# Recurrent attention and expert layer on one core: where the first group's small steps run, and when the second group's x is made

## The chip, the cores and the metric

The kernel runs on one core of a Trainium2 chip. Its time is the device time of one execution in microseconds, the median of several runs. The engines are TensorE (PE in the profile, with its weight loads as PEld), VectorE (DVE), ScalarE (ACT), GpSimd (POOL) and SyncE (SP, which here only issues DMAs). Each takes its instructions in order.

## The reference

```python
def _attn_ref(q, k, v, alpha):               # (4, 8, 768, 48) each
    ...
    for t in range(S):
        state = alpha[:, :, t, :, None] * state + np.einsum('bhd,bhe->bhde', k[:, :, t], v[:, :, t])
        y[:, :, t] = np.einsum('bhd,bhde->bhe', q[:, :, t], state)

def _moe_ref(x, domain_probs, w1, w2):       # x (3072, 384), 4 experts, F = 1024
    p = domain_probs / (domain_probs.sum(-1, keepdims=True) + 1e-09)
    for e in range(E):
        h = np.maximum(x @ w1[e], 0.0)
        out += p[:, e:e + 1] * (h @ w2[e])
```

x is the attention's y with heads side by side, (batch, position) as rows. Everything is float32.

## The kernel before

The 768 positions of each of the 4 batches are cut into 6 blocks of 128, which gives 24 units, taken block by block: unit u is block u // 4 of batch u % 4. Units are put together into groups whose x feeds the expert layer at once: the first group holds units 0 and 1, the second units 2 to 5, and so on in fours, with two left for the last. For each group, four experts are run; each has an `up` stage (x times w1, in eight chunks of 128 hidden columns) and a `down` stage (hidden times w2). The attention of the next group's units is dealt out between these matmuls: `deal` gives each of a unit's steps (the stretches between `yield`s) a due time by a table of costs, and `advance` emits the steps that are due. The emission order is the order on each engine.

A unit (`attention`) first transposes alpha, k and q on TensorE (`turned`, L270). ScalarE copies the first two out of PSUM as AT (L281) and KT (L286); VectorE multiplies the third by AT into QT (L293). `own` and `dot` (L289, L290) are the terms of each position with itself. Then come seven levels, m = 1, 2, 4 ... 64. At each, ScalarE copies one half of QT into a block of its own, qb (`copy_q`, L312, two instructions); VectorE multiplies that half by the decay of its neighbour (`next_q`, L319) and makes the next level's decay (L321); and `next_k` makes the next level's K: the right halves are copied unchanged (L330, ScalarE), the left halves are multiplied by the decay (L331, VectorE). There are six such copies a unit. The K tiles rotate over five buffers. TensorE's `products` (L338) give the scores of a level, which VectorE puts into `near` under a mask (L348); `far` (L393) is the last level. ScalarE copies both into `lat` (L406 for far, L410 for near, two instructions each, one for each half of the partitions). `result` (L432) multiplies lat by v, adds the state's part where there is an earlier block, and leaves x; `turn_keys` (L456) and the state's update (L467 to L476) follow.

From the second group on, x is taken in three parts, top, low and dif, so that matmuls of a faster type can be used. `split_x` makes them, at four points of the last `down` before the group's first `up`: step 0 makes all the top parts on ScalarE (L502), and steps 1 to 3 make low and dif of one third each on VectorE (`split_rest`, L252 and L253). The points are shares of that `down`: 0.0, 0.6, 0.7 and 0.78. Beside the first group the weights are split likewise (`split_piece`, L226 to L232) and the parts stored to DRAM by DMAs from GpSimd's queue (L233); `load_piece` reads them back for later groups (L196) and reads the raw weights (L214, L215 for w1, L217 for w2), all on SP's queue. GpSimd has no other work behind the memsets of the start but the stores of finished rows (L675).

At the start, SP's queue issues unit 0's loads (alpha, k, q and three for v), unit 1's, and the first four pieces of w1. ScalarE's queue issues the identity, the masks and the probabilities `p_all`. TensorE runs fillers, matmuls of zeros that nobody reads (L749): eight before the first step, and then so many behind each step of units 0 and 1 as the list in the code says. `norm_probs` follows at the end of that list.

Of the kernel before, what the change touches and what calls it, by code (L numbers as in the profile page):

```python
# [10 lines left out]
F32 = mybir.dt.float32  # L11
# [5 lines left out]
AX = mybir.AxisListType  # L17
# [3 lines left out]
def kernel(  # L21
# [37 lines left out]
    nc = tc.nc  # L59

    B, H, S, D = q.shape
    E, DM, F = moe_w1.shape
    P = 128
# [7 lines left out]
    NT = B * P  # L71
# [11 lines left out]
    n = np.arange(QUAD)[None, :]  # L83
# [7 lines left out]
    work = ctx.enter_context(tc.tile_pool(name="work", bufs=2))  # L91
# [7 lines left out]
    p_all = const.tile([P, NBLK, E], F32, name="p_all")  # L99
# [3 lines left out]
    near = const.tile([P, H, HALF], F32, name="near")  # L103
    lat = const.tile([P, H, P], F32, name="lat")
# [7 lines left out]
    half = B // 2  # L112
# [18 lines left out]
    def raw(u, nm):  # L131
        return values[u % 2] if nm == "v" else apart[nm] if u == 1 else early[nm]
# [27 lines left out]
    def load(u, names):  # L160
        if u >= len(units):
            return
        cb, b = units[u]
        for nm in names:
            src = srcs[nm][b, :, cb * P:(cb + 1) * P, :].rearrange("h s d -> s h d")
            if nm != "v":
                nc.sync.dma_start(out=raw(u, nm)[:, :, :D], in_=src)
                continue

            pairs = raw(u, nm).rearrange("p (a i) d -> p a i d", i=2)  # L170
            src = src.rearrange("p (a i) d -> p a i d", i=2)
            nc.sync.dma_start(out=pairs[:, :, 0, :D], in_=src[:, :, 0])
            nc.sync.dma_start(out=pairs[:, :, 1, :TAIL], in_=src[:, :, 1, QUAD:])
            nc.sync.dma_start(out=pairs[:, :, 1, TAIL:D], in_=src[:, :, 1, :QUAD])
# [81 lines left out]
    def norm_probs():  # L256
        nc.vector.reduce_sum(out=tot, in_=p_all, axis=AX.X)
        nc.vector.tensor_scalar_add(out=tot, in0=tot, scalar1=1e-9)
        nc.vector.reciprocal(out=tot, in_=tot)
        nc.vector.tensor_mul(p_all, p_all, tot.unsqueeze(2).broadcast_to([P, NBLK, E]))  # L260
        nc.vector.tensor_scalar_mul(out=p_fine, in0=p_all, scalar1=FINE)


    def halves(t, m):
        return t.rearrange("p a (b two r) -> p a b two r", two=2, r=m)

    def turned(src):
        tp = ps.tile([P, NP, P], F32, name="tp", tag="w")
        for p in range(NP):
            nc.tensor.transpose(tp[:, p, :], src(p), ident)  # L270
        return tp

    def attention(u):
        cb, b = units[u]
        ra, rk, rq, rv = (raw(u, nm) for nm in ("a", "k", "q", "v"))
# [6 lines left out]
        after = u + 2 if u == 0 else u + 1 if u > 1 else len(units)  # L282
# [1 line left out]
        yield  # L284
        KT = keys()
        nc.scalar.copy(out=KT, in_=turned(pair(rk)))  # L286
        own = work.tile([P, NT], F32, name="t")[:, :H * D].rearrange("p (h d) -> p h d", d=D)
        dot = work.tile([P, H], F32, name="dot")
        nc.vector.tensor_mul(own, rq[:, :, :D], rk[:, :, :D])  # L289
        nc.vector.reduce_sum(out=dot, in_=own, axis=AX.X)  # L290
        load(after, "k")
        yield
        nc.vector.tensor_mul(QT, turned(pair(rq)), AT)  # L293
        load(after, "q")
        yield

# [27 lines left out]
        def next_k(li):  # L324
            m = LEVELS[li]
            old = new = halves(KTs[li], m)
            if li + 1 < len(LEVELS):
                KTs.append(keys())
                new = halves(KTs[-1], m)
                nc.scalar.copy(out=new[:, :, :, 1, :], in_=old[:, :, :, 1, :])  # L330
            nc.vector.tensor_mul(new[:, :, :, 0, :], old[:, :, :, 0, :],  # L331
                                 spread(halved(decs[li])[:, :, :, 1], m))

# [23 lines left out]
        for li in range(3):  # L357
            copy_q(li)
            next_q(li)
            next_k(li)  # L360
            yield
# [6 lines left out]
        for li in range(4):  # L368
            products(li, banks[li // 2][:, li % 2])
        next_q(3)  # L370
        next_k(3)
        take(0, banks[0][:, 0])
        take(1, banks[0][:, 1])
        yield
        copy_q(4)
        next_q(4)
        next_k(4)
        take(2, banks[1][:, 0])
        take(3, banks[1][:, 1])
# [24 lines left out]
        for s in range(2):  # L404
            rows = slice(HALF * s, HALF * (s + 1))
            nc.scalar.copy(out=parts[:HALF, :, s, :, HALF:], in_=far[rows])  # L406
        yield
        for s in range(2):
            rows = slice(HALF * s, HALF * (s + 1))
            nc.scalar.copy(out=lat[rows, :, rows], in_=near[rows])  # L410
        KT = KTs[-1]
        yield

# [49 lines left out]
        if cb < NCB - 1:  # L463
# [5 lines left out]
            for i in range(2):  # L469
                rows = slice(HD * i, HD * (i + 1))  # L470
                old, add = st[rows, :, i, :], sps[rows, :, i, :]
# [208 lines left out]
    def cost(layer, gi, e):  # L680
        n = len(groups[gi]) / 4
        if layer == 0:
            return 2.1 * n if split1(gi, e) else 2.6 * n
        return 4.1 if gi > 1 else 4.7 if split2(gi, e) else 5.4
# [32 lines left out]
    def advance(spent):  # L717
        nonlocal clock
        clock += spent
        while waiting and clock >= waiting[0][0]:  # L720
            next(waiting.popleft()[2], None)

    with tc.manual_schedule():
        nc.scalar.dma_start(out=ident_all, in_=nc.inline_tensor(ident_np, name="ident_c").ap())
        nc.scalar.dma_start(out=masks, in_=nc.inline_tensor(mask_np, name="masks_c").ap())
        nc.scalar.dma_start(out=p_all, in_=moe_domain_probs.rearrange("(n p) e -> p n e", p=P))
        nc.gpsimd.memset(sts[B - 1], 0.0)
        for nm in "akq":
            for r in (early[nm], apart[nm]):
                nc.gpsimd.memset(r[:, :, D:], 0.0)  # L730
        nc.gpsimd.memset(lat[HALF:, :, :HALF], 0.0)
        for t in values + blocks:
            nc.gpsimd.memset(t, 0.0)
        for t in sts[:-1]:
            nc.gpsimd.memset(t, 0.0)

        load(0, "akqv")
        load(1, "akqv")
        for i in range(NQ):
            load_piece(0, i)  # L740

        idle = ps.tile([P, P], F32, name="idle", tag="g", bufs=4)
        zeros = sts[B - 1].rearrange("p a i d -> p (a i d)")[:, :P]

        def fill(n):
            for _ in range(n):
                nc.tensor.matmul(idle, lhsT=zeros, rhs=zeros, start=True, stop=True)  # L749

        runs = [attention(u) for u in range(len(groups[0]))]
        fill(8)
        for u, n in ((0, 3), (0, 6), (0, 4), (0, 5), (0, 5), (0, 4), (0, 3), (1, 0), (0, 0), (0, 2),
                     (0, 2), (1, 2), (0, 2), (1, 0), (0, 0), (0, 4), (0, 4), (0, 0)):
            next(runs[u])
            fill(n)
        norm_probs()

        span = cost(0, 0, 0) * FCH / 2 + cost(1, 0, 0)
        waiting.extend((span * (k + 1) / 15, u, runs[u])  # L760
                       for k, u in enumerate([1, 1, 1, 0, 1, 0, *[1] * 8]))
        for fc in range(FCH):
            up(0, 0, fc, slice(0, 1))
            advance(cost(0, 0, 0) / 2)
        down(0, 0, [0], deque())
        while waiting:
            next(waiting.popleft()[2], None)
        clock = 0.0
        waiting.extend((1.0 + k, 1, runs[1]) for k in range(2))
        waiting.extend(deal())  # L770

        for (gi, e), after in zip(tasks, [*tasks[1:], (None, None)]):
            rest = gi == e == 0
            for fc in range(FCH):
                up(gi, e, fc, slice(1, len(groups[0])) if rest else None)
                advance(cost(0, gi, e) / (2 if rest else 1))
            each = len(groups[gi]) if split2(gi, e) else 1
            turns = [range(k, k + each) for k in range(rest, len(groups[gi]), each)]
            for k, slots in enumerate(turns):

                between = deque()
                if after[1] == 0:
                    for step, at in enumerate((0.0, 0.6, 0.7, 0.78)):
                        at = at * len(turns) - k
                        if 0 <= at < 1:
                            between.append((at, lambda step=step: split_x(after[0], step)))
                down(gi, e, slots, between)
        while stores:
            stores.popleft()()
# [28 lines left out]
```

## Time and profile before

| | us |
|---|---|
| median of 8 runs | 1063.61 |
| lowest, highest | 1060.66, 1064.84 |
| the profiled execution | 1063.43 |
| its span, first to last instruction | 1061.7 |
| mean granted TensorE clock | 0.998 |

The span is what the profile's tables are made of; the profiled execution's own time is 1.73 us longer. A line of the profile that begins with an engine (or with the time) names the source line, the operation, what is written and what is read, and how often; in square brackets is the idle time of the engine just before it, with what ended it. Matmuls of float32 show up as two instructions each.

| of the span | busy us | share |
|---|---|---|
| PE | 1041.1 | 98% |
| PE's weight loads | 905.7 | 85% |
| DVE | 781.1 | 74% |
| ACT | 568.6 | 54% |
| POOL | 32.7 | 3% |

### The profile page before, as it was taken

The page shows a single profiled execution, that of the slowest core. Times are in us where ns is not written, and L with a number is a line of the kernel's source. Part 1 is how long each engine was busy: PE and PEld are TensorE (multiplying, and loading weights), DVE is VectorE, ACT ScalarE, POOL GpSimd, SP SyncE. Part 2 cuts the span into 40 slices and gives each one's busy share as a digit, 9 for nine tenths or more (in the row PEclk, how much of TensorE's full clock was granted, in tenths as well). Part 3 has the DMA queues.
Part 4 walks back from the last instruction along what each step waited for, and adds up shares of the span by engine and source line. Part 5 has one row for each costly group of instructions (what it writes and reads, how often), then busy time and mean ns, then how long its engine had stood idle before and what let it go on. Part 6 is the DMA issues. An engine that isn't in the chain of part 4 may idle for free.

```text
span 1061.7 us, 21599 instructions
## 1 busy us (share of the span) xinstructions
PE 1041.1 (98%) x8508; PEld 905.7 (85%) x8508; DVE 781.1 (74%) x1619; ACT 568.6 (54%) x1202; POOL 32.7 (3%) x71
## 2 busy tenths in 40 slices
PE   8899999999999999999999999999999999999998
PEld 8777776687878798898898998988989889898988
DVE  5488777677779877778877877986878776666565
ACT  5687875675756555536446535555564543423232
POOL 2010010000001000000000000000000000000000
PEclk9999999999999999999999999999999999999999
DMA  8596699797877958658669558585694554544531
GB/s 124 158 326 208 237 314 350 275 347 240 303 253 274 379 174 285 274 158 328 235 197 362 194 205 333 165 320 222 173 363 173 209 209 152 205 179 179 192 166 45
DMA packets 158837, 251.66 MB, mean 237 GB/s; under 512 B 120112, under 2 KB 135344, under 8 KB 136208
## 3 DMA queue, kind: packets, MB, share of 16 engines
q1 hardware_dynamic: 149600, 208.82, 57.4%
q0 software_dynamic: 5760, 41.29, 9.7%
q8 instruction: 67, 1.10, 0.4%
q10 hardware_dynamic: 3376, 0.17, 0.3%
q14 instruction: 34, 0.28, 0.1%
HBM read 207.79 MB, written 42.47 MB: 236 GB/s over the span
## 4 chain that ended last, share of the span: by engine, by line
PE 85%; DVE 5%; ACT 5%; DMA 2%; issue 2%; SPq 0%; ACTq 0%; DVEq 0%
PE ops L639 36%; PE one L546 23%; PE two L546 11%; PE sc L338 6%; PE yps L432 3%; PE tp L270 3%; ACT qb L312 2%; PE one L538 2%; PE sps L467 1%; PE far L393 1%; DMA hT<-in_moe_w_dram 1%; DVE near L348 1%; DVE w L230 1%; ACT KT L330 1%; DMA rq<-in_q_dram 1%
## 5 line engine op out<-in xcount | busy, mean ns | idle before, releaser
L639 PE MATMUL ops<-w,hT 128*128 128x384 f32 x1872 | 346.4, 340 | 0.2 <-DVE hT L592 0.2
L639 PEld LDWEIGHTS ops<-w,hT 128*128 128x128 f32 x1872 | 324.3, 188 | 4.7 <-ACT t L557 0.6
L546 PE MATMUL one<-xT,w 128*128 128x512 f32 x960 | 253.9, 399 | 2.7 <-DVE xT L252 2.3
L546 PEld LDWEIGHTS one<-xT,w 128*128 128x128 f32 x960 | 176.2, 189 | 41.9 <-DVE xT L252 4.0
L557 ACT ACTIVATE t<-one 128x512 f32<-128x512 f32 (+1 forms) x192 | 107.0, 557 | 179.9 <-PE one L546 174.9
L312 ACT COPY qb<-QT 64x256 f32<-64x256 f32 x336 | 136.6, 406 | 71.1 <-DVE QT L293 42.5
L586 DVE SCALAR_TENSOR_TENSOR hT<-t,hT 128x512 fp32r<-128x512 f32 (+1 forms) x172 | 110.4, 642 | 68.3 <-ACT hT L584 66.1
L559 DVE TENSOR_TENSOR t<-t,two 128x512 f32<-128x512 f32 (+1 forms) x172 | 109.3, 636 | 57.8 <-ACT t L557 29.3
L584 ACT ACTIVATE hT<-t 128x512 fp32r<-128x512 f32 (+1 forms) x172 | 101.8, 592 | 86.3 <-DVE t L559 85.3
L546 PE MATMUL two<-xT,w 128*128 128x512 f32 x480 | 136.8, 393 | 0.0
L546 PEld LDWEIGHTS two<-xT,w 128*128 128x128 f32 x480 | 90.4, 189 | 20.1 <-DVE acc L668 0.2
L639 PE MATMUL ops<-hT 128*128 128x384 f32 x288 | 100.9, 491 | 0.4 <-DMA hT<-in_moe_w_dram 0.4
L592 DVE SCALAR_TENSOR_TENSOR hT<-hT 128x512 fp32r<-128x512 f32 (+1 forms) x172 | 100.9, 633 | 0.0
L348 DVE COPY_PREDICATED near<-masks,sc 128x256 f32<-128x256 uint8 x144 | 76.8, 533 | 19.4 <-PE sc L338 16.7
L319 DVE TENSOR_TENSOR QT<-QT,dec 128x256 f32<-128x256 f32 x144 | 60.8, 422 | 36.0 <-ACT qb L312 35.3
L338 PEld LDWEIGHTS sc<-qb,KT 128*64 128x64 f32 x2304 | 72.7, 138 | 9.3 <-issue 4.7
L338 PE MATMUL sc<-qb,KT 128*64 128x64 f32 x2304 | 77.2, 223 | 2.6 <-ACT qb L312 2.6
L639 PEld LDWEIGHTS ops<-hT 128*128 128x128 f32 x288 | 52.1, 190 | 29.8 <-DMA hT<-in_moe_w_dram 1.1
L668 DVE SCALAR_TENSOR_TENSOR acc<-ops,p_all,acc 128x384 f32<-128x384 f32 x82 | 49.9, 614 | 30.2 <-PE ops L639 29.1
L330 ACT COPY KT<-KT 128x256 f32<-128x256 f32 x144 | 60.0, 416 | 3.2
L331 DVE TENSOR_TENSOR KT<-KT,dec 128x256 f32<-128x256 f32 x144 | 60.1, 418 | 0.0
L538 PE MATMUL one<-xT,w 128*128 128x256 f32 (+1 forms) x240 | 46.2, 340 | 0.6 <-ACT xT L448 0.6
(88 smaller groups left out, 935.4 us busy)
## 6 DMA issues: line engine op xcount, KB each, us to landing
w<-kept SPq DMA_DIRECT2D x144, 1152.0 KB
kept<-w POOLq DMA_DIRECT2D x32, 1152.0 KB, 7.3
hT<-in_moe_w_dram SPq DMA_DIRECT2D x32, 384.0 KB
w<-in_moe_w_dram SPq DMA_DIRECT2D x48, 128.0 KB
ra<-in_alpha_dram SPq DMA_DIRECT2D x23, 192.0 KB
rk<-in_k_dram SPq DMA_DIRECT2D x23, 192.0 KB
rq<-in_q_dram SPq DMA_DIRECT2D x23, 192.0 KB
out_dram<-acc POOLq DMA_DIRECT2D x18, 192.0 KB, 7.6
```

Of the source, the lines that this page charges most:

```text
L312: nc.scalar.copy(out=qb[rows, :, i, :].rearrange("p a (b r) -> p a b r", r=m), in_=qv[rows])
L330: nc.scalar.copy(out=new[:, :, :, 1, :], in_=old[:, :, :, 1, :])
L338: nc.tensor.matmul(out[HALF * s:HALF * (s + 1), 2 * p:2 * p + 2, :], lhsT=KTs[li][:, p, HALF * s:HALF * (s + 1)], rhs=qbs[li][:, p, :, QUA ...
L348: nc.vector.copy_predicated(near.rearrange("p a (b two r) -> p a b two r", two=2, r=m)[:, :, :, 1, :], mk.unsqueeze(1).broadcast_to([P, H, ...
L538: nc.tensor.matmul(one, lhsT=w[:, kc], rhs=xraws[gi][:, kc, lo:hi], start=(kc == 0), stop=(kc == KC - 1))
L546: nc.tensor.matmul(out, lhsT=w[:, part, kc], rhs=x_part(gi, part, kc), start=(part == terms[0] and kc == 0), stop=(part == terms[-1] and k ...
L557: nc.scalar.activation(out=t, in_=one, func=ACT.Copy, scale=FINE)
L559: nc.vector.tensor_add(t, t, two)
L584: nc.scalar.activation(out=top, in_=x, func=ACT.Relu, scale=TRIM)
L586: nc.vector.scalar_tensor_tensor(out=low, in0=x, scalar=0.0, in1=top.bitcast(F32), op0=ALU.max, op1=ALU.subtract)
L592: nc.vector.scalar_tensor_tensor(out=dif, in0=top.bitcast(F32), scalar=1 / 4096.0, in1=low.bitcast(F32), op0=ALU.mult, op1=ALU.subtract)
L639: nc.tensor.matmul(sums[at], lhsT=h, rhs=w, start=(n == begins[at]), stop=(n == ends[at]))
```

## The change

Six edits. In the first unit (`alone`), own and dot are emitted behind QT and not ahead of it, with the load of k for a later unit that follows them, and the second of lat's two copies of near goes to VectorE. For units 0 to 5 (`dense`: those that run ahead of or beside the first group), the copy of K's right halves goes from ScalarE to GpSimd. The load of p_all goes from ScalarE's queue to SP's, behind the loads of units 0 and 1 and ahead of the first pieces of w1. The fillers are 7, 2 and 3 instead of 8, 3 and 6 at the first three places. And steps 1 to 3 of `split_x` come at 0.3, 0.42 and 0.54 of the first group's last `down`; for later groups they stay where they were.

```diff
         dot = work.tile([P, H], F32, name="dot")
-        nc.vector.tensor_mul(own, rq[:, :, :D], rk[:, :, :D])
-        nc.vector.reduce_sum(out=dot, in_=own, axis=AX.X)
-        load(after, "k")
+        def own_terms():
+            own = work.tile([P, NT], F32, name="t")[:, :H * D].rearrange("p (h d) -> p h d", d=D)
+            nc.vector.tensor_mul(own, rq[:, :, :D], rk[:, :, :D])
+            nc.vector.reduce_sum(out=dot, in_=own, axis=AX.X)
+            load(after, "k")
+        alone = u == 0
+        dense = u < half + B
+        if not alone:
+            own_terms()
         yield
         nc.vector.tensor_mul(QT, turned(pair(rq)), AT)
+        if alone:
+            own_terms()
         load(after, "q")
...
-                nc.scalar.copy(out=new[:, :, :, 1, :], in_=old[:, :, :, 1, :])
+                copy = nc.gpsimd.tensor_copy if dense else nc.scalar.copy
+                copy(out=new[:, :, :, 1, :], in_=old[:, :, :, 1, :])
...
-            nc.scalar.copy(out=lat[rows, :, rows], in_=near[rows])
+            copy = nc.vector.tensor_copy if alone and s else nc.scalar.copy
+            copy(out=lat[rows, :, rows], in_=near[rows])
...
-        nc.scalar.dma_start(out=p_all, in_=moe_domain_probs.rearrange("(n p) e -> p n e", p=P))
...
         load(0, "akqv")
         load(1, "akqv")
+        nc.sync.dma_start(out=p_all, in_=moe_domain_probs.rearrange("(n p) e -> p n e", p=P))
         for i in range(NQ):
             load_piece(0, i)
...
-        fill(8)
-        for u, n in ((0, 3), (0, 6), (0, 4), (0, 5), (0, 5), (0, 4), (0, 3), (1, 0), (0, 0), (0, 2),
+        fill(7)
+        for u, n in ((0, 2), (0, 3), (0, 4), (0, 5), (0, 5), (0, 4), (0, 3), (1, 0), (0, 0), (0, 2),
                      (0, 2), (1, 2), (0, 2), (1, 0), (0, 0), (0, 4), (0, 4), (0, 0)):
...
-                    for step, at in enumerate((0.0, 0.6, 0.7, 0.78)):
+                    for step, at in enumerate((0.0, 0.3, 0.42, 0.54) if gi == 0 else
+                                              (0.0, 0.6, 0.7, 0.78)):
```

More of the change, by code (lines that the diff above doesn't have):

```diff
@@ L286, in attention @@
         nc.scalar.copy(out=KT, in_=turned(pair(rk)))
-        own = work.tile([P, NT], F32, name="t")[:, :H * D].rearrange("p (h d) -> p h d", d=D)
         dot = work.tile([P, H], F32, name="dot")
-        nc.vector.tensor_mul(own, rq[:, :, :D], rk[:, :, :D])
-        nc.vector.reduce_sum(out=dot, in_=own, axis=AX.X)
-        load(after, "k")
+        def own_terms():
[7 more added lines that the diff above has]
+            own_terms()
         yield
         nc.vector.tensor_mul(QT, turned(pair(rq)), AT)
+        if alone:
+            own_terms()
         load(after, "q")
```

## The prediction

> **What bounds the kernel now.** The page's first part comes first: TensorE is busy for 98% of the span, so the question is where the missing 20 us lie. The table by stage (columns: window and length, PE, PEld, DVE, ACT, POOL busy with instruction counts, granted clock, DMA share, GB/s), with its limits at the first matmul of the expert layer, at the end of the first group and after the second group's start, answers it.
>
> ```profile
> PE 1041.1 (98%) x8508; PEld 905.7 (85%) x8508; DVE 781.1 (74%) x1619; ACT 568.6 (54%) x1202; POOL 32.7 (3%) x71
> ```
> ```profile
> 0.00:26.36 26.36, 22.36 (x269) 21.20 (x269) 13.93 (x39) 14.02 (x30) 5.92 (x21) 1.00 0.84 124
> 26.36:60.00 33.64, 29.94 (x297) 24.52 (x298) 19.40 (x44) 23.29 (x58) 1.53 (x3) 1.00 0.66 181
> 60.00:163.80 103.80, 97.60 (x999) 75.22 (x998) 81.72 (x183) 80.67 (x178) 7.13 (x15) 1.00 0.83 277
> 163.80:176.00 12.20, 10.37 (x36) 7.21 (x35) 9.13 (x20) 4.40 (x10) 1.06 (x2) 0.86 0.97 374
> 176.00:1061.70 885.70, 880.79 (x6913) 777.56 (x6911) 656.92 (x1335) 446.18 (x928) 17.10 (x32) 1.00 0.65 236
> ```
>
> After 176 us TensorE idles 4.9 of 886 us, and the change touches nothing there: whatever is won before 176 us should arrive whole at the end. Before it, 4.0 us are idle in the first 26.36 us (where part of the busy time is the filler of L749, too), 3.7 + 6.2 us in the rest of the first group, and 1.8 us at the second group's start, at a mean granted clock of only 0.86.
>
> Next, the timeline of the start, on TensorE and VectorE. It shows what the first unit waits for.
>
> ```profile
> 1.21 3.78 PE L749 MATMUL idle<-st 128*128 128x128 f32 x16 [1.21 <-POOL st L727]
> 4.78 1.06 PE L270 MATMUL tp<-ident,ra 128*128 128x128 f32 x4
> 6.35 0.60 PE L270 MATMUL tp<-ident,rk 128*128 128x128 f32 x4
> 6.79 1.50 PE L749 MATMUL idle<-st 128*128 128x128 f32 x12
> 8.80 0.63 PE L270 MATMUL tp<-ident,rq 128*128 128x128 f32 x4 [0.51 <-DMA rq<-in_q_dram]
> ...
> 8.77 0.56 DVE L289 TENSOR_TENSOR t<-rq,rk 128x384 f32<-128x384 f32 x1 [8.77 <-DMA rq<-in_q_dram]
> 9.83 0.68 DVE L293 TENSOR_TENSOR QT<-tp,AT 128x512 f32<-128x512 f32 x1
> ```
>
> The transposes of ra and rk follow the filler without a gap; that of rq waits for its load. The product QT at L293 then waits a little more, for own and dot (L289, L290) ahead of it on VectorE.
>
> Last, TensorE's timeline at the second group's start, and the clock there.
>
> ```profile
> 165.99 0.49 PE L546 MATMUL one<-xT,w 128*128 128x512 f32 x1 [0.18 <-DVE xT L252]
> 167.31 0.51 PE L546 MATMUL one<-xT,w 128*128 128x512 f32 x1 [0.83 <-DVE xT L252]
> 168.64 1.34 PE L546 MATMUL one<-xT,w 128*128 128x512 f32 x4 [0.82 <-DVE xT L252]
> ```
> ```profile
> 168.00:170.00 2.00, 1.36 (x5) 0.89 1.01 424
> 170.00:172.00 2.00, 2.00 (x8) 0.50 1.02 431
> 172.00:174.00 2.00, 2.00 (x8) 0.76 0.99 279
> ```
>
> Three stalls on the pieces of x add to 1.83 us, and right after them the granted clock is at half.
>
> **The change, part by part.** The sum is made against the profiled execution's own 1063.43 us (span 1061.7); the median of the runs is 1063.61, 0.18 above it.
>
> 1. *p_all leaves ACT's queue; fewer fillers; own and dot behind QT.* p_all is 128 x 24 = 3,072 rows of 16 bytes, most of the 3,376 packets of q10. The DMA view of 0 to 10 us counts 9,123 packets, with the engines saturated from 1.75 us: 0.90 us a thousand. p_all therefore takes 2.8 us of the engines while rq is on its way; without it rq could land at 8.77 - 2.8 = 6.0. If the queues did not share the engines, it would gain nothing. TensorE's fillers then gate: one fewer of the first eight saves 0.25 to 0.47 (3.78 / 8; I take 0.4), one of three 0.25, three of six 0.75 (1.50 / 2). The rq transposes start at 8.80 - 0.51 - 1.40 = 6.9 at the earliest, 1.9 us sooner. QT could have begun at 9.5, when its transposes were done, but began at 9.83: another 0.33. Sum -2.23, and between -0.33 and -2.5. What it moves: own and dot (0.56 + 0.55) run while ACT copies qb for 0.86 us and VectorE sat idle for 0.98, so they cost nothing; uncovered they'd cost 1.1. On SP's queue the issue of k's load for the third unit stays between those of a and q. p_all's issue now stands ahead of twelve issues of w1; by DMA time these move back 2.8 us at the end of the same saturated stretch that p_all leaves shorter, so they land as before. The last was issued at 23.15 and its piece is read by the seventh of eight chunks, near 31 us: covered by some 4 us even with a start 2.5 us sooner.
>
> 2. *lat's second half on VectorE (first unit).* ACT's two copies of L410 take 1.25 us together from 23.38. VectorE does its half behind the KT product that ends at 23.66, so near 24.2 both are done. But the eight fillers ahead of yps end at 24.37, where yps began at 24.68: -0.3.
>
> 3. *GpSimd's 36 KT copies.* Each took ACT 0.41 us (0.33 from start to start) and lies in ACT's queue in front of what TensorE waits for. The PE waits between 20 and 180 us name ACT:
>
> ```profile
> PE yps L432 <- ACT lat L410: 3.1, 4, 1.4
> PE far L393 <- ACT qb L312: 2.9, 2, 1.6
> PE sc L338 <- ACT qb L312: 2.6, 3, 1.2
> ```
>
> In ACT's timeline a KT copy stands in the unbroken row just ahead of the awaited copy in five of the long ones (those that end at 33.0, 63.6, 80.2, 84.0 and 121.3 us): 5 x 0.33 = -1.65. The far waits are set by VectorE (qb 6 waits for QT), and gain nothing. If the row ahead merely re-forms it is half, -0.8; if each earlier copy helps too, up to -3.
>
> Against it stands GpSimd's own price p. No row shows a GpSimd copy. Its memsets give 204 ns for 128x128 and 540 ns for 128x512, so some 0.32 for 256 columns that are only written; twice that, 0.64, if reading is added in full. ACT needs 0.41. I take p = 0.5. Nor does a row show VectorE beside a reading GpSimd: memsets end before VectorE's first instruction. So the blocking is between zero and all of p that no idle time covers. Copy 0 needs only the transposed K. Copies 4 and 5 lie beside the near updates (1.49 and 0.89 us). Copies 1 and 2 end in the 0.3 us that VectorE waits for qb, and cost up to p - 0.3 each; copy 3 has no such gap, up to p: 0.9 us a unit. On the path that counts whole for the first two units and, by my estimate, a quarter for each of the four others, which have matmuls to cover them: up to 3 x 0.9 = 2.7. I take half: +0.45 at the start and +0.9 beyond it.
>
> The rule that speaks against this part is in the Trainium skill, SBUF — State Buffer, section "Who interferes with whom": a VectorE instruction with two SBUF inputs and a GpSimd instruction that reads SBUF exclude each other. The QT, dec and KT products are of that kind; by the rule the blocking is the whole 2.7 and the result 1.35 us later than my sum, by the rows alone anything from zero. No run so far shows it.
>
> On POOL's queue the copies share with the weight stores of L233, which wait there for VectorE's L232 (76.3 us of waits in five of them). A KT copy behind such a store waits for it plus its 0.53 us issue. VectorE's next KT product comes 1.2 us after L232 (QT, dec and KT go first), so the cover holds for p up to 0.7.
>
> 4. *x from 0.30.* The pieces come one turn earlier. VectorE's 3 x (0.68 + 0.69) us are the same work, moved from 165.25 to some 156 to 163 us. ACT's top part is ready at 156.2. VectorE idles 0.53 and 0.91 us there. The unit's own work slides behind, into the time the pieces leave free. TensorE arrives at 165.8 and finds all three: -1.83 of stalls. What is slow behind them is counted by rows: four transposes take 1.06 us (0.60 elsewhere, from start to start 0.42 more), six matmuls of one 2.19 (1.56), three of two 1.49 (0.86): -1.68. Together -3.5; if only the stalls go, -1.8.
>
> Sum: -2.23 - 0.3 + 0.45 - 1.65 + 0.9 - 3.5 = -6.3. 1063.43 - 6.3 + 0.18 = **1057.3**.
>
> **Rivals.** *Slower: GpSimd's copy is long, and VectorE waits for each.* The gains without blocking are 2.53 + 1.65 + 3.5 = 7.7 us. Blocking costs 3 x (2(p - 0.3) + p) = 9p - 1.8, so it decides from p = 1.06 us on. At p = 1.5 it is 11.7, and the kernel 4 us slower: 1067.6. For it: strided elements in runs as short as one. Against it: p would be three times the interpolated memset. 9%.
>
> *The transfers hold the time.* SP's queue issues without a break from 139.4 to 189 us at a DMA share near 1:
>
> ```profile
> 155.61 17.53 SPq L196 DMA_DIRECT2D w<-kept  x4
> 174.55 5.32 SPq L217 DMA_DIRECT2D hT<-in_moe_w_dram  x2
> ```
>
> The fourth w piece, issued by 173.1, is read at 184.5; w2's last, issued by 182.5, after 195. With some 3 us from issue to landing (my estimate; POOL's stores of the same size took 7.3 in all) 5 us or more are left, hardly 2 after moving the readers up by 3.5. Were there none, part 4 is lost: 1060.8; if the earlier gain is absorbed too, 1063.6. 16%.
>
> *rq does not land sooner*, because another transfer in the same queue held it. Part 1 shrinks to 0.33, the sum to -4.4: 1059.2. 12%.
>
> **How the numbers follow.** The forecast has 63%. A difference of 0.2%, 2.1 us, is about what this kernel's runs can tell from no change. Its own bounds reach from -9.3 (1054.3) to about -0.5 (part 1 alone failing with full blocking and only the stalls won). 1053.8 to 1061.8 takes in the third rival, most of the forecast and half of the second. Faster: 0.61 + 0.12 + 0.08 = 0.81; within 0.2%: 0.02 + 0.08 = 0.10; slower 0.09.
>
> **What would show it.** Right: rq's transposes near 6.9, QT near 7.6, the first matmul of L538 near 24.3 us; no xT wait, and clock 1.00, at the second group's start, which lies near 163.0 instead of 165.99. GpSimd rows of about 0.5 us, VectorE's L319 starting 0.1 to 0.3 us later behind qb. Wrong: copies near 1 us, or a new DMA wait at L546 or L639.

## The result and the profile after

The changed kernel takes 1058.01 us (median of 13 runs, 1056.81 to 1062.93) where the kernel before takes 1062.63 (median of 37, 1060.66 to 1065.77). The ratio is 0.9957, with a 95% interval from 0.9948 to 0.9966: faster by 4.6 us, between 3.6 and 5.5. A second set of runs of the same kernel, beside the last experiments, gave 0.9951 (0.9939 to 0.9964). The forecast was 1057.3, a gain of 6.3 us over the 1063.61 that the kernel before had in its first eight runs. The profiled execution takes 1056.87 us with a span of 1054.8. Lines have moved: the filler is L762, the expert matmuls L551 (first group) and L559, K's copy L342, QT L302 and L330, the products L350, yps L445, far L405.

The table by stage of the kernel after, with limits that follow the same events:

```profile
0.00:24.30 24.30, 21.21 (x258) 20.15 (x258) 14.79 (x40) 11.20 (x23) 9.34 (x28) 1.00 0.79 116
24.30:58.00 33.70, 30.70 (x300) 24.70 (x302) 19.82 (x45) 21.31 (x51) 4.36 (x9) 1.00 0.69 191
58.00:161.00 103.00, 97.69 (x998) 75.37 (x999) 85.43 (x184) 73.64 (x154) 17.52 (x36) 1.00 0.86 281
161.00:173.00 12.00, 11.90 (x82) 9.09 (x82) 9.13 (x23) 7.22 (x16) 1.61 (x3) 1.00 0.92 364
173.00:1054.80 881.80, 876.83 (x6872) 774.50 (x6868) 654.81 (x1331) 443.30 (x922) 17.10 (x32) 1.00 0.66 237
```

TensorE idles 0.1 us at the second group's start, where it idled 1.8, and the clock there is whole. Behind it, it idles 5.0 us (4.9 before). ACT's busy time from the first expert matmul to 161 us has gone down and POOL's up.

The start on TensorE and VectorE, and the second group's first matmuls:

```profile
7.18 0.60 PE L270 MATMUL tp<-ident,rq 128*128 128x128 f32 x4
7.90 0.69 DVE L302 TENSOR_TENSOR QT<-tp,AT 128x512 f32<-128x512 f32 x1 [7.90 <-PE tp L270]
...
24.33 3.62 PE L551 MATMUL one<-xT,w 128*128 128x128 f32 x30 [0.59 <-ACT xT L461]
...
162.87 1.62 PE L559 MATMUL one<-xT,w 128*128 128x512 f32 x6
```

rq's transposes now follow the filler without a wait, QT waits for nothing but them, and no stall on x stands in front of L559. The waits of TensorE between 20 and 180 us:

```profile
PE yps L445 <- ACT lat L423: 2.1, 2, 1.1
PE far L405 <- ACT qb L323: 1.3, 1, 1.3
PE sc L350 <- ACT qb L323: 1.2, 2, 0.9
PE sc L350 <- DVE w L230: 1.1, 1, 1.1
...
PE one L551 <- DMA w<-in_moe_w_dram: 0.7, 1, 0.7
```

The first three were 3.1, 2.9 and 2.6, but those take in the first unit's waits on far (1.37) and yps (0.31). The first unit's wait on far is nearly as long as it was (1.32) and now lies ahead of 20 us. From the first expert matmul on, yps waited 2.8, far 1.6 and sc 2.6 before. The last two lines are new. GpSimd's copies and VectorE beside them, in the first unit (two views):

```profile
12.17 0.40 POOL L342 COPY KT<-KT 128x256 f32<-128x256 f32 x1 [0.94 <-DVE KT L343]
13.26 0.68 DVE L376 TENSOR_TENSOR near<-ident,dot 128x512 f32<-128x512 f32 x1
13.47 0.73 POOL L342 COPY KT<-KT 128x256 f32<-128x256 f32 x1 [0.90 <-DVE KT L343]
13.86 0.62 DVE L330 TENSOR_TENSOR QT<-QT,dec 128x256 f32<-128x256 f32 x1
```

A copy takes 0.40 us by itself. The one that meets two products of VectorE takes 0.73, and the second of these products 0.62 where 0.41 to 0.45 is usual.

### The profile page after: what moved, and what is told of

It reads as the page before. It is cut to its first block, busy times and chain, and to the rows that moved or that the text cites. A ratio compares the mean times of both kernels' runs of the same rounds, so it can differ in the third digit from the quotient of the medians.

```text
span 1054.8 us, 21607 instructions
## 1 busy us (share of the span) xinstructions
PE 1038.3 (98%) x8498; PEld 903.8 (86%) x8498; DVE 784.0 (74%) x1620; ACT 556.7 (53%) x1165; POOL 49.9 (5%) x107
## 4 chain that ended last, share of the span: by engine, by line
PE 88%; DVE 4%; ACT 3%; DMA 2%; SPq 1%; issue 1%; POOL 0%; ACTq 0%; DVEq 0%; POOLq 0%
PE ops L652 37%; PE one L559 23%; PE two L559 11%; PE sc L350 6%; PE tp L270 3%; PE yps L445 3%; PE one L551 2%; PE sps L480 1%; PE far L405 1%; DMA hT<-in_moe_w_dram 1%; ACT qb L323 1%; SPq L214 1%; DMA w<-in_moe_w_dram 1%; DVE w L230 1%; ACT lat L423 0%
## 5 line engine op out<-in xcount | busy, mean ns | idle before, releaser
L559 PE MATMUL one<-xT,w 128*128 128x512 f32 x960 | 252.6, 398 | 1.0 <-DVE xT L252 0.5
L559 PEld LDWEIGHTS one<-xT,w 128*128 128x128 f32 x960 | 175.7, 188 | 39.5 <-ACT t L570 1.5
L559 PE MATMUL two<-xT,w 128*128 128x512 f32 x480 | 136.2, 392 | 0.0
L559 PEld LDWEIGHTS two<-xT,w 128*128 128x128 f32 x480 | 90.1, 188 | 20.0 <-DVE acc L681 0.3
L330 DVE TENSOR_TENSOR QT<-QT,dec 128x256 f32<-128x256 f32 x144 | 61.8, 429 | 33.2 <-ACT qb L323 32.6
L350 PEld LDWEIGHTS sc<-qb,KT 128*64 128x64 f32 x2304 | 72.9, 138 | 9.0 <-issue 6.3
L350 PE MATMUL sc<-qb,KT 128*64 128x64 f32 x2304 | 77.5, 223 | 2.3 <-ACT qb L323 1.2
L551 PE MATMUL one<-xT,w 128*128 128x256 f32 (+1 forms) x240 | 46.7, 341 | 1.4 <-DMA w<-in_moe_w_dram 0.7
L342 ACT COPY KT<-KT 128x256 f32<-128x256 f32 x108 | 44.9, 416 | 2.3
```

Of the source, the lines that this page charges most:

```text
L330: nc.vector.tensor_mul(qv, qv, spread(dv[:, :, :, 0], m))
L350: nc.tensor.matmul(out[HALF * s:HALF * (s + 1), 2 * p:2 * p + 2, :], lhsT=KTs[li][:, p, HALF * s:HALF * (s + 1)], rhs=qbs[li][:, p, :, QUA ...
L551: nc.tensor.matmul(one, lhsT=w[:, kc], rhs=xraws[gi][:, kc, lo:hi], start=(kc == 0), stop=(kc == KC - 1))
L559: nc.tensor.matmul(out, lhsT=w[:, part, kc], rhs=x_part(gi, part, kc), start=(part == terms[0] and kc == 0), stop=(part == terms[-1] and k ...
```

## The experiments

Every kernel was timed in five rounds beside the kernel before. Ratios are to it.

**Part 4 alone, on the kernel before.**

```diff
-                    for step, at in enumerate((0.0, 0.6, 0.7, 0.78)):
+                    for step, at in enumerate((0.0, 0.3, 0.42, 0.54) if gi == 0 else
+                                              (0.0, 0.6, 0.7, 0.78)):
```

> The kernel before with one edit: steps 1 to 3 of split_x at 0.3, 0.42 and 0.54 of the first group's last down. Theory (the sum of the prediction): the three stalls of 1.83 us go and with them the half clock behind them, 1.68 us, so 3.5 us less than the kernel before in the same rounds (near 1059.1). Rival (the clock dip is a matter of one execution's phase, the stalls are not): 1.8 us less, near 1060.8. Second rival (transfers hold the time): under 0.5 us less, and a DMA wait at the first matmuls of the second group's up or down.

Measured: 1060.55 us, ratio 0.9977 (0.9968 to 0.9985), so 2.4 us less, between 1.6 and 3.4. The stalls on x are gone; a wait of 0.3 us for the parts of w from DRAM stands there instead. The value lies between the theory's and the first rival's. The mean clock that is listed with each execution fits this (half clock for 3.4 us costs 1.7 of some 1062 us, which gives 0.998): 14 of the 23 executions of the kernel before in these rounds ran at 0.998, and their median is 1063.77; the nine others, at 0.999 or 1.000, have 1062.16. None of the 11 of this kernel ran at 0.998. Against the nine without the dip the gain is 1.6 us, against the fourteen with it 3.2.

**All but part 4.**

```diff
-                    for step, at in enumerate((0.0, 0.3, 0.42, 0.54) if gi == 0 else
-                                              (0.0, 0.6, 0.7, 0.78)):
+                    for step, at in enumerate((0.0, 0.6, 0.7, 0.78)):
```

> The changed kernel with steps 1 to 3 of split_x back at 0.6, 0.7 and 0.78 for every group. Theory: it keeps the 2.0 us of the start and the 0.9 us of the rest of the first group, so 2.9 us less than the kernel before (near 1059.7), and shows the three stalls and a clock of about 0.86 at the second group's start again. Rival (the parts depend on one another: a first group that is done sooner meets x even later): the stalls are longer than 1.83 us in sum and the kernel is less than 2 us ahead of the kernel before.

Measured: 1059.62 us, ratio 0.9973 (0.9965 to 0.9981), 2.9 us less: the theory's number. The stalls are back in its profile, and in this execution the half clock as well (TensorE's timeline, then windows of 2 us: busy time, clock, DMA share, GB/s):

```profile
164.08 0.50 PE L559 MATMUL one<-xT,w 128*128 128x512 f32 x1 [0.72 <-DVE xT L252]
165.41 2.07 PE L559 MATMUL one<-xT,w 128*128 128x512 f32 x4 [0.83 <-DVE xT L252]
```
```profile
164.90:166.90 2.00, 1.49 (x4) 0.57 0.98 414
166.90:168.90 2.00, 2.00 (x8) 0.57 1.04 437
```

Of its 12 executions four ran at 0.998 (median 1061.32, the rest 1059.36). The dip is not in every execution that has the stalls.

**Fillers in the stalls, on the kernel before.** This takes most of TensorE's idleness there away and leaves the wait for x (zeros gets a tile of its own).

```diff
                     for kc in range(KC):
+                        if gi == 1 and e == fc == 0 and part == 1 and kc > 0:
+                            for _ in range(3):
+                                nc.tensor.matmul(two[:, :P], lhsT=zeros, rhs=zeros, start=True, stop=True)
```

> The kernel before with three fillers (matmuls of zeros that nobody reads, 0.7 us) in each of the two long stalls on x at the second group's start, so that TensorE is busy while it waits for VectorE. Theory formed on the runs so far: the stalls cost 1.8 us in every execution, but the half clock behind them comes only in some (clock 0.998 in 14 of 23 runs of the kernel before, median 1063.8; the other nine 1062.2); with the idle time filled no execution shows 0.998, and the median is that of the nine, 1062.2, some 0.6 us less than the kernel before. Theory of the prediction (the half clock is there in every execution of the kernel before): 1.7 us less, near 1061.1. Rival (the dip has another cause than these stalls): about half of the executions still at 0.998 and no gain.

Measured: 1062.96 us, ratio 0.9992 (0.9984 to 1.0001). None of the 11 executions ran at 0.998; of the 24 of the kernel before beside them, 15 did (median 1064.06, the others 1062.72). In its profile the clock stays whole, though a wait of 0.69 us for w stands ahead of the first matmul:

```profile
167.33 0.83 PE L549 MATMUL two<-zeros 128*128 128x128 f32 x6
168.23 0.83 PE L549 MATMUL two<-zeros 128*128 128x128 f32 x6
```
```profile
167.03:169.03 2.00, 2.00 (x14) 1.00 1.01 429
169.03:171.03 2.00, 1.90 (x10) 1.00 0.98 412
```

So the idle pieces make this dip, and only in some executions: the revised theory holds by the count (0 of 11 against 15 of 24). Its 0.6 us are not shown by the time, whose interval includes no change.

**GpSimd's copies alone, on the kernel before.**

```diff
-                nc.scalar.copy(out=new[:, :, :, 1, :], in_=old[:, :, :, 1, :])
+                copy = nc.gpsimd.tensor_copy if u < half + B else nc.scalar.copy
+                copy(out=new[:, :, :, 1, :], in_=old[:, :, :, 1, :])
```

> The kernel before with GpSimd's copies of K's right halves for units 0 to 5 as the only edit. Theory of the prediction: -1.65 for ScalarE's waits and +1.35 for the blocking of VectorE, so 0.3 us less than the kernel before, with the start 0.2 to 0.4 us later and the second group 0.9 us sooner behind the first expert matmul. Rival (it is worth nothing, since the waits re-form on VectorE): within 0.3 us of the kernel before at an equal clock, with the second group no sooner behind the first expert matmul than 139.6 us.

Measured: 1062.90 us, ratio 0.9999 (0.9989 to 1.0008). In the profile the first expert matmul comes at 26.60 (26.36 before) and the second group 138.74 us later (139.63 before): both steps as the theory had them. The time does not tell 0.3 us from nothing.

**GpSimd's copies undone, on the changed kernel**, in two sets of rounds.

```diff
-                copy = nc.gpsimd.tensor_copy if dense else nc.scalar.copy
+                copy = nc.scalar.copy
                 copy(out=new[:, :, :, 1, :], in_=old[:, :, :, 1, :])
```

> The changed kernel with the right halves of K copied by ScalarE for all units, as before. Theory: the first group's waits for ScalarE come back (0.9 us from the first expert matmul to the second group), the blocking of VectorE in the first unit goes (0.3 us), so 0.6 us more than the changed kernel (near 1058.6). Rival (GpSimd's copies cost more by blocking VectorE than they take off ScalarE): 0.5 to 1 us less than the changed kernel.

> The changed kernel with all copies of K's right halves on ScalarE, beside the changed kernel in the same rounds. Theory: GpSimd's copies win 0.9 us between the first expert matmul and the second group (138.5 against 139.5 us in the profiles) and cost 0.2 us in the first unit, so this kernel is 0.7 us slower than the changed one. Rival (the first timed comparison, 1057.74 against 1058.01 us, is right): within 0.3 us of it.

> The changed kernel itself, for a comparison in the same rounds with the three others. Theory: 4.6 us less than the kernel before, as measured, with a clock of 0.998 in few of its executions.

Measured: first 1057.74 us (ratio 0.9953, 0.9940 to 0.9965), not told apart from the changed kernel, whose runs were others. In the second set 1058.74 (0.9965, 0.9952 to 0.9977) beside 1056.98 for the changed kernel in the same rounds (0.9951, 0.9939 to 0.9964): 1.8 us apart by the medians, but the intervals overlap. The profiles agree with one another: from the first expert matmul to the second group it is 140.46 and 140.58 us with ScalarE's copies, 138.54 and 139.12 with GpSimd's. What comes back are the waits on ScalarE that the prediction had named (second set, 24 to 170 us; both were 2.1 and 1.2 in the changed kernel of the same rounds):

```profile
PE yps L445 <- ACT lat L423: 2.6, 2, 1.4
PE sc L350 <- ACT qb L323: 2.6, 3, 1.2
```

Part of the gain turned into a new wait: in the changed kernel the products wait 1.1 us for VectorE behind a weight split (L230), which is in neither of the other two profiles. The other profiles agree: it is 138.5 to 139.1 us in all six with GpSimd's copies (for units 2 to 5 at least) and without norm_probs or lat moved (changed kernel twice, no_split, kt_alone, kt_from_u2, p_all_first), and 139.4 to 140.6 in all five with ScalarE's (before, split_alone, stall_filled, and these two). By the profiles the copies help; by how much, between nothing and 1.8 us, the times leave open.

**GpSimd's copies from the third unit on.**

```diff
-        dense = u < half + B
+        dense = half <= u < half + B
```

> The changed kernel with GpSimd's copies for units 2 to 5 only; the first two units copy on ScalarE as before. Theory: the first expert matmul comes 0.3 us sooner (24.0 instead of 24.33), since VectorE isn't blocked in the first unit, and the rest keeps ScalarE's relief: 0.3 us less than the changed kernel. Rival (the copies are worth most in units 0 and 1, where TensorE has least to cover the waits with): 0.5 us more than the changed kernel, with longer waits on lat and qb before 60 us.

Measured: 1058.00 us, ratio 0.9959 (0.9945 to 0.9973), the same as the changed kernel. The first expert matmul came at 24.85, since QT began at 8.60: in this execution the transposes of ra and rk took 1.09 and 1.06 us, against 1.09 and 0.60 in the changed kernel's profile and 0.63 each in that of its second set. From QT on it took 16.25 us against 16.43. The two profiles with all copies on ScalarE have 16.25 and 16.23, the five others with GpSimd's copies and qb on ScalarE 16.44 to 16.47: the copies cost the first unit 0.2 us. The way to the second group (138.73 us) is as short as with the copies in all six units, although the rival's longer waits in the second unit are there (far 1.57 instead of 1.32, yps 0.15 where there was none). The rival's 0.5 us is not seen, nor are the theory's 0.3; the interval, some 1.5 us to either side, excludes neither.

**p_all back on ScalarE's queue, on the changed kernel.**

```diff
         nc.scalar.dma_start(out=masks, in_=nc.inline_tensor(mask_np, name="masks_c").ap())
+        nc.scalar.dma_start(out=p_all, in_=moe_domain_probs.rearrange("(n p) e -> p n e", p=P))
...
-        nc.sync.dma_start(out=p_all, in_=moe_domain_probs.rearrange("(n p) e -> p n e", p=P))
```

> The changed kernel with the load of p_all back on ScalarE's queue behind the masks, fillers and all else as changed. Theory: rq lands near 8.8 us again, its transposes start there, QT at 9.5, and the first expert matmul near 26.0 instead of 24.33: 1.6 us more than the changed kernel. Rival (it was the fillers that held the start): rq's transposes start before 7.7 us, and the time is within 0.4 us of the changed kernel.

Measured: 1060.12 us, ratio 0.9978 (0.9968 to 0.9988), 2.1 us above the changed kernel by medians of different rounds; the first expert matmul comes at 26.03, 1.7 us later than the changed kernel's 24.33. TensorE waits for rq again:

```profile
8.85 0.63 PE L270 MATMUL tp<-ident,rq 128*128 128x128 f32 x4 [1.49 <-DMA rq<-in_q_dram]
```

The theory's 8.8, 9.5 (9.59 measured) and 26.0 all came. p_all is what held rq; moving it is the largest single gain of the start. QT follows 0.74 us behind the start of rq's transposes here, too, where it was 1.03 before: this 0.3 us comes from own and dot behind QT.

**p_all behind w1, on the changed kernel.**

```diff
-        nc.sync.dma_start(out=p_all, in_=moe_domain_probs.rearrange("(n p) e -> p n e", p=P))
         for i in range(NQ):
             load_piece(0, i)
+        nc.sync.dma_start(out=p_all, in_=moe_domain_probs.rearrange("(n p) e -> p n e", p=P))
...
-        norm_probs()
...
+        norm_probs()
         down(0, 0, [0], deque())
```

> The changed kernel with the load of p_all on SP's queue behind the first four pieces of w1 and not ahead of them, and norm_probs emitted behind the first unit's up. Theory: the wait of 0.71 us on w at the seventh chunk of the first up (30.0 us) comes from p_all's 3,072 packets ahead of the pieces, so it goes: 0.7 us less than the changed kernel (near 1057.3), first expert matmul at 24.3 us as before. Rival (the pieces are held by their own rate on SP's queue, and the first unit is merely done too soon for them): the wait stays at 0.5 to 0.9 us and the time does not move by more than 0.3 us.

Measured: 1059.22 us, ratio 0.9966 (0.9954 to 0.9978). The wait for w is gone, as the theory has it, but its 0.7 us are not: the time is no better. norm_probs, moved with the load, now lies in VectorE's row for the second unit, and far waits longer (VectorE's timeline, then TensorE's):

```profile
35.09 0.22 DVE L257 TENSOR_REDUCE tot<-p_all 128x24 f32<-128x96 f32 x1
36.19 0.21 DVE L261 TENSOR_SCALAR p_fine<-p_all 128x96 f32<-128x96 f32 x1
39.29 1.12 PE L405 MATMUL far<-qb,KT 128*64 128x128 f32 x8 [2.24 <-ACT qb L323]
```

Five small instructions from 35.09 to 36.40 stand there for 1.2 us; far waits 2.24 instead of 1.32, and a wait of 1.0 us of the state's matmuls on ScalarE takes the place of that for w. Two of the six executions ran at 0.998, the profiled one among them: its clock is 0.76, 0.50 and 0.89 in the windows of 2 us from 38 to 44 us, at the end of far's wait and behind it. What the wait for w is worth by itself is not settled: the edit moved two things.

**lat's second half on GpSimd; qb's second half, too.**

```diff
-            copy = nc.vector.tensor_copy if alone and s else nc.scalar.copy
+            copy = nc.scalar.copy if not (dense and s) else nc.vector.tensor_copy if alone else nc.gpsimd.tensor_copy
```

and for the second kernel, besides, qb's rows of the second head (`i == 1`) on GpSimd and K's right halves on ScalarE while u < half.

> The changed kernel with the second of lat's two copies of near on GpSimd for units 1 to 5 (the first unit's stays on VectorE). Theory: what TensorE still waits for before the second group is ScalarE's row of copies; two waits of yps for lat (1.0 and 1.06 us) fall by 0.5 us each as both halves are copied at once, so 1.0 us less than the changed kernel. Rival (the wait moves to qb, which ScalarE copies next, or GpSimd's half ends later than ScalarE's two did): within 0.4 us of it.

> As the one before, and in the first two units the second of the two copies of qb goes to GpSimd while K's right halves stay on ScalarE there. Theory: the first unit's levels follow one another every 1.41 us, set by ScalarE's two qb copies (0.86) and VectorE's QT (0.43); with the copies side by side a level takes 1.2 to 1.3 us, bound by VectorE's three products, so the first expert matmul comes 0.3 to 0.5 us sooner, and the time is 1.3 to 1.5 us below the changed kernel's. Rival (VectorE was the bound from the fourth level on, and GpSimd's reading holds its products): the first expert matmul no sooner than 24.2 us and no gain over the kernel with lat on GpSimd alone.

Measured: 1060.54 us (0.9982, 0.9973 to 0.9991) and 1059.04 (0.9971, 0.9960 to 0.9983), both slower than the changed kernel in the same rounds (1056.98, no execution above 1058.39; the fastest of these two kernels took 1059.56 and 1058.75). Neither the theory of the first nor its rival came. The copy itself took 0.67 us on average, but it stood behind a weight store on POOL's queue, which waits for VectorE (kernel with lat alone; POOL's timeline, then TensorE's):

```profile
119.28 0.53 POOL L233 DMA_DIRECT2D kept<-w  x1 [4.28 <-DVE dec L332]
119.85 0.61 POOL L423 COPY lat<-near 64x512 f32<-64x512 f32 x1
120.52 0.56 PE L445 MATMUL yps<-lat,rv 128*32 128x128 f32 x8 [3.96 <-POOL lat L423]
```

One wait of 4.0 us, where the changed kernel waits 1.06; and with it the half clock (0.67, 0.50 and 0.98 in the windows of 2 us from 120 to 126 us); all 11 executions of this kernel have 0.996 to 0.998. The part on qb went as expected: VectorE's QT products follow one another after 1.24 and 1.07 us in place of 1.41, and from QT to the first expert matmul it takes 15.85 us instead of 16.43 (16.2 with K's copies alone back on ScalarE). qb on GpSimd without lat is what this points to; it wasn't tried.

## Why the prediction was right, and where it was not

*What bounds it.* Right: what was won before 176 us arrived, and the idle time behind it stayed at 5 us. The forecast time is 0.7 us below the measured one, but the forecast gain is 1.7 us too large and lies outside the measured 3.6 to 5.5: the other 1.0 us is the kernel before, whose median over 37 runs is 1062.63, not 1063.61.

*Part 1.* Right in each step: transposes at 7.18 (6.9 forecast), QT at 7.90 (7.6), first expert matmul at 24.33 (24.3). The load's cause is shown by undoing it (+2.1 us). One sentence failed: the pieces of w1 were to "land as before". Their last issue ended at 24.05 instead of 23.15, TensorE waited 0.71 us for w until 29.99, and its weight loads waited again until 30.55, some 6 us behind that issue. The forecast's own numbers leave 31 - 2.5 - 23.15 = 5.4 us, so its 4 us of cover allowed only 1.4 us from issue to landing.

*Part 2.* The fillers bound yps, as forecast: they ended at 22.66 and yps followed. No run takes this edit alone.

*Part 3.* p was taken as 0.5; alone it is 0.40, over all 36 copies 0.48. VectorE's QT product at levels 2 to 6 took 450 ns on average instead of 425, at level 1 467 instead of 423, near's product 738 instead of 683. That is 40 x 25 + 7 x 44 + 7 x 55 ns = 1.7 us up to 163 us, and the decay, KT and own products add some 1.5 us (the decay product of 128x32, for one, 239 ns instead of 183). Little of it reached the path: from QT on, the first unit took 0.2 us longer with the copies than without (0.45 was forecast). The middle, 24.33 to 162.87 us, is 1.1 us shorter than before; 0.75 was forecast. In the five places that the prediction named (by their ends in the kernel before) TensorE's idle time fell by 0.57, 0.30, 0.18, 0.16 and 0.37 us, 1.58 in all against -1.65, but not by 0.33 each, and in part by luck: the first (1.28, now 0.71 for w) is shorter with ScalarE's copies, too, and in the fourth 1.05 us on VectorE took the place of 1.21 on ScalarE. The far wait, which was to gain nothing, fell from 1.56 to 1.32. The page of the Trainium skill that spoke against this part (SBUF — State Buffer, "Who interferes with whom") holds in kind: both engines lose time where they meet. The full price, 0.9 us a unit, was not paid on the path, where the first unit lost 0.2. The slower rival needed p over 1.06 us.

*Part 4.* Here the sum failed: "-1.68" for the half clock was counted as if it came in every execution of the kernel before, because it was in the profiled one. Over the 63 executions of the kernel before beside the experiments, 32 ran at 0.998 with a median of 1063.96, 31 without the dip with 1062.38. The dip costs 1.6 us, as sized, but in half of the cases: 0.8 on average. With that, part 4 is 1.83 + 0.8 = 2.6 instead of 3.5 (2.4 measured alone), and the forecast 5.4, within the measured 3.6 to 5.5. The prediction had the smaller case, "if only the stalls go, -1.8", as a bound only.

*The rivals.* Transfers did not hold the time: 0.3 to 0.8 us of waits on w from DRAM show in some profiles at the second group's start, no more. One of the two profiles of the changed kernel has such a wait (0.57), which the prediction had named as a sign of being wrong. rq did land sooner.

## What to carry to other kernels

When a stage is bound by one engine, price each stall there from its own rows, and ask of each cost behind it whether it comes in every execution: one profile is one draw, and the clock that is listed for each run tells how often. A small load of many tiny rows can hold the one load that everything waits for; here its place in the queues was worth 1.7 us at the start, where own and dot behind QT, and lat's second half on VectorE, brought 0.3 each by the profiles. An idle engine is not a free one: what matters is what else waits in its queue, and a copy behind a store that waits for VectorE can cost more than it takes off.

## What was not expected of the hardware

Three idle pieces, of 0.2, 0.8 and 0.8 us within 2.8 us in the profiled execution, bring the half clock in about half of the executions of the kernel before (32 of 63). It came with one piece of 4.0 us in all 11 executions of one kernel, and with fillers that keep TensorE busy in none (0 of 11). With the other two kernels that have the stalls (no_split 4 of 12, kt_alone 7 of 11) it is 43 of 86. The Trainium skill (TensorE: Matmul & The Clock Gate, "HAM oscillation — how this bites in real kernels") puts its rule at idle gaps above some 3.4 us; these runs show that shorter pieces in a row can be enough, and the runs decide. Where the half clock comes at the second group's start, it lasts 3.4 us in the profiled executions (0.89, 0.50 and 0.76 in windows of 2 us, in the prediction: 0.22 + 1.00 + 0.48 = 1.7 us of full clock lost, which at half clock takes twice that). The changed kernel has none of these stalls, and yet one of its 19 listed executions ran at 0.998, its slowest (1062.93), and one of five with the copies from the third unit on (1061.08); what they met is not known. The length of the first matmuls varies, too: the transposes of ra took 1.09 us in one execution of the changed kernel and 0.63 in another, and QT began between 7.65 and 8.60 us in the nine profiles in which rq is loaded ahead of p_all.
